# One-core pruned-weight matmul: another queue for the first token pair, one load in place of two for the first 512 weight columns, and a rewritten opening order

## The chip, the core and the metric

The kernel runs on one NeuronCore of a Trainium2 chip. The metric is the device time of one launch in microseconds (us). The kernel before was timed in three runs: 233.45, 233.73 and 233.89 us, median 233.73 us.

A core has five instruction streams that run side by side and meet only at semaphores: TensorE (PE in the profile, its weight loads PEld), VectorE (DVE), ScalarE (ACT), GpSimd (POOL) and SyncE (SP). SP, ACT and POOL can each issue DMA transfers; the transfers of all three run on the same 16 DMA engines.

## The reference

```python
def reference(x, w, b):                  # x 16x512x1024, w 1024x1024, b 1024, all bf16
    wg = w.reshape(G, M, D)              # M = 4 neighbouring rows of w form a group
    mag = jnp.abs(wg)
    order = jnp.argsort(mag, 1)
    thr = jnp.take_along_axis(mag, order[:, M - N:M - N + 1, :], 1)   # N = 2: the second largest
    mask = mag >= thr
    wp = (wg * mask).reshape(D, D)
    return jnp.einsum("bsd,df->bsf", x, wp) + b
```

In each column of w, out of every four neighbouring rows the two with the largest magnitudes are kept and the others become zero. Then 8192 tokens are multiplied by the pruned weights and the bias is added.

## The kernel before

**Tiles.** The 8192 tokens are 64 tiles of 128. The contraction (1024) is split in two halves g of 512, the output columns in two halves h of 512. A weight tile `w_gh[(g, h)]` has 128 partitions, 4 rows m (the four rows of a group, so that pruning works along the free dimension) and 512 columns. Pruning goes by six *pieces* (line 61): pieces 0 to 3 are the four 256-column quarters of g = 0, pieces 4 and 5 the two 512-column halves of g = 1.

**Pruning a piece.** `abs_piece` (lines 107 to 120) takes the magnitudes, on DVE or, with `on_act`, on ACT. `prep_piece` (lines 122 to 144) runs on DVE: maximum and minimum of row pairs (`hi`, `lo`, lines 129 and 130), three more to reach the threshold (lines 133, 134, 136), then the mask (line 142) and the product that overwrites w (line 144). For pieces 0 and 1 mask and product are done in two halves of two rows each, first both masks, then both products.

**The opening.** The first eight token tiles cannot wait for DMA transposes. They are loaded in pairs (`load_x`, line 76, 256 KB each), transposed on PE against an identity matrix (line 161; the identity is made on POOL, line 100), copied from PSUM to SBUF by ACT (`copy_half`, line 166), and multiplied by the pruned w where it lies (line 182). While the first loads are on their way, PE multiplies zeros (`warm`, line 103).

**The loads** are issued in the order of lines 83 to 90, and later ones by the order below. SP and ACT each issue their own list, one after another:

```python
    load_w(0, 0, 256, nc.sync, 0, 2)
    load_w(0, 0, 256, nc.scalar, 2, 4)
    load_x(0, 2)
    load_x(2, 4, nc.scalar)
    load_x(4, 6)
    load_w(0, 256, 512)
    load_x(6, 8)
    load_w(0, 512, 1024)
```

**The order.** `K` keeps the program order, so each engine executes its own instructions in the order in which they are written. The string `FRONT` (lines 256 to 268) writes the first tokens' work out by hand. Its words: W and w, a matmul of zeros with 512 or 128 columns; A.i and P.i, magnitudes and pruning of piece i; T.t and C.t, transposes of token tile t (four instructions) and its copy by ACT; M.i.t, the four matmuls of tile t with piece i; N.i.t.m.., only those of the rows m; V, a copy of a finished half sum from PSUM to SBUF on ACT; U, DMAs that move pruned w to the layout of the rest of the kernel (line 151); I, a weight load; D, G, L, DMA transposes of later tokens; X, Y, O, B, Q, the sums of the later front tiles, their additions and the bias load. All engines get their parts of this one list.

**The rest.** From line 328 on, 50 token tiles are multiplied by the whole pruned w, 16 matmuls of 512 columns each (line 338; the last tile by line 234), and DVE adds the bias while it empties PSUM (line 219).

Of the kernel before, what the change touches and what calls it, by code (L numbers as in the profile page):

```python
# [10 lines left out]
def kernel(  # L11
# [7 lines left out]
    nc = tc.nc  # L19
    P = 128  # L20
# [7 lines left out]
    B, S, D = x.shape  # L28
# [10 lines left out]
    T, F = 8, 6  # L39
# [13 lines left out]
    def next_bank():  # L53
        bk = nbk[0] % 8
        nbk[0] += 1
        return bk
# [8 lines left out]
    def w_of(i):  # L65
        g, c0, c1 = pieces[i]
        return w_gh[(g, c0 // FH)][:, :, c0 % FH:c0 % FH + c1 - c0]

    def load_w(g, c0, c1, eng=nc.sync, m0=0, m1=4):
        dst = w_gh[(g, c0 // FH)][:, m0:m1, c0 % FH:c0 % FH + c1 - c0]  # L70
        K(eng.dma_start(dst, wv[:, g, m0:m1, c0:c1]))  # L71
# [4 lines left out]
    def load_x(ta, tb, eng=nc.sync):  # L76
        xt = const.tile([P, tb - ta, KH], bf16, name=f"xh_{ta}")
        src = xf[ta * P:tb * P, 0:KH].rearrange("(t p) c -> p t c", p=P)
        K(eng.dma_start(xt[:], src))  # L79
        for t in range(ta, tb):  # L80
            xh[t] = xt[:, t - ta, :]

    load_w(0, 0, 256, nc.sync, 0, 2)
    load_w(0, 0, 256, nc.scalar, 2, 4)
    load_x(0, 2)
    load_x(2, 4, nc.scalar)
    load_x(4, 6)
    load_w(0, 256, 512)
    load_x(6, 8)
    load_w(0, 512, 1024)  # L90
    bias_sb = const.tile([P, Dout], bf16, name="bias_sb")
# [10 lines left out]
    def warm(n):  # L102
        K(nc.tensor.matmul(bank[7][:, :n], lhsT=zeros[:, :P], rhs=zeros[:, :n], start=True, stop=True))  # L103
# [3 lines left out]
    def abs_piece(i, on_act):  # L107
        g, c0, c1 = pieces[i]
        n = c1 - c0
        if n <= 256:  # L110
            mag = mags_pool.tile([P, 4, n], bf16, name="mag")[:]
        else:
            mag = mag2_pool.tile([P, 4, n], bf16, name="mag2")[:]
        if on_act:
            K(nc.scalar.activation(mag, w_of(i), Act.Abs))
        else:
            for ms in (slice(0, 2), slice(2, 4)) if i == 0 else (slice(0, 4),):
                K(nc.vector.tensor_single_scalar(  # L118
                    mag[:, ms].bitcast(u16), w_of(i)[:, ms].bitcast(u16), 0x7FFF, op=Alu.bitwise_and))
        mags[i] = mag  # L120

    def prep_piece(i):
        g, c0, c1 = pieces[i]
        n = c1 - c0
        mag = mags.pop(i)
        magv = mag.rearrange("p (a j) f -> p a j f", j=2)
        hi = tmp.tile([P, 2, FH], bf16, name="hi")[:, :, :n]
        lo = tmp.tile([P, 2, FH], bf16, name="lo")[:, :, :n]
        K(nc.vector.tensor_tensor(hi, magv[:, :, 0, :], magv[:, :, 1, :], op=Alu.max))
        K(nc.vector.tensor_tensor(lo, magv[:, :, 0, :], magv[:, :, 1, :], op=Alu.min))  # L130
        t1 = tmp.tile([P, FH], bf16, name="t1")[:, :n]
        t2 = tmp.tile([P, FH], bf16, name="t2")[:, :n]
        K(nc.vector.tensor_tensor(t1, hi[:, 0, :], hi[:, 1, :], op=Alu.min))
        K(nc.vector.tensor_tensor(t2, lo[:, 0, :], lo[:, 1, :], op=Alu.max))
        thr = tmp.tile([P, FH], bf16, name="thr")[:, :n]
        K(nc.vector.tensor_tensor(thr, t1, t2, op=Alu.max))
        mask = tmp.tile([P, 4, FH], bf16, name="mask")[:, :, :n]

        halves = (slice(0, 2), slice(2, 4)) if i < 2 else (slice(0, 4),)
        for ms in halves:  # L140
            tb = thr[:, None, :].to_broadcast([P, ms.stop - ms.start, n])
            K(nc.vector.tensor_tensor(mask[:, ms], mag[:, ms], tb, op=Alu.is_ge))  # L142
        for ms in halves:
            K(nc.vector.tensor_tensor(w_of(i)[:, ms], w_of(i)[:, ms], mask[:, ms], op=Alu.mult))  # L144

    wp_nat = [const.tile([P, KT, FH], bf16, name=f"wp_nat{h}") for h in range(2)]

# [8 lines left out]
    def transpose_half(t):  # L156
        own[(0, t)] = next_bank()
        xv = xh[t].rearrange("p (q m) -> p m q", m=4)
        dst = bank[own[(0, t)]][:].bitcast(bf16)[:, :4 * P].rearrange("p (m q) -> p m q", m=4)
        for m in range(4):  # L160
            K(nc.tensor.transpose(dst[:, m, :], xv[:, m, :], ident[:]))  # L161

    def copy_half(t):
        xt = const.tile([P, 4, P], bf16, name=f"xT_{t}")
        src = bank[own[(0, t)]][:].bitcast(bf16)[:, :4 * P].rearrange("p (m q) -> p m q", m=4)
        K(nc.scalar.copy(xt[:], src))  # L166
        xT[t] = xt


    def mm_part(q, t, c0, c1, ms=range(4)):  # L170
        g, h = divmod(q, 2)
        if c0 == 0 and (q > 0 or t >= T) and 0 in ms:
            own[(q, t)] = next_bank()
        dst = bank[own[(q, t)]][:, c0:c1]
        for m in ms:
            if t >= T:
                lhs, rhs = xN[t][:, 4 * g + m, :], wp_nat[h][:, 4 * g + m, c0:c1]
            elif g == 0:
                lhs, rhs = xT[t][:, m, :], w_gh[(0, h)][:, m, c0:c1]
            else:  # L180
                lhs, rhs = xg1[:, m, t * P:(t + 1) * P], wp_nat[h][:, 4 + m, c0:c1]
            K(nc.tensor.matmul(dst, lhsT=lhs, rhs=rhs, start=c0 == 0 and m == 0, stop=c1 == FH and m == 3))  # L182
# [45 lines left out]
    def load_fill(g):  # L228
        src = xf[T * P:(T + F) * P, g * KH:(g + 1) * KH]
        K(nc.sync.dma_start_transpose(out=xfill[:, 4 * g:4 * g + 4, :], in_=src))  # L230
# [6 lines left out]
    def issue_batch(t0, nb):  # L237
# [16 lines left out]


    FRONT = """
        I.1.0.512 D.0 A.0 P.0 W W W W W W W W w w T.0 T.1 C.0 T.2 T.3 C.1 w T.4 T.5 C.2 N.0.0.0 N.0.0.1 N.0.1.0
        N.0.1.1 N.0.0.2 N.0.0.3 N.0.1.2 N.0.1.3 A.1 C.3 P.1 U.0.0.0.512 I.1.512.1024 G C.4 M.0.2 C.5 M.0.3 T.6 T.7
        C.6 M.0.4 C.7 A.2 M.0.5 M.0.6 P.2 M.0.7 M.1.0 A.3 M.1.1 M.1.2 M.1.3 V.0.0 M.1.4 V.0.1 M.1.5 V.0.2 M.1.6
        V.0.3 M.1.7 V.0.4 P.3 M.2.0 V.0.5 M.2.1 V.0.6 M.2.2 V.0.7 M.2.3 M.2.4 M.2.5 M.2.6 A.4 P.4 U.1.0.0.512 D.1  # L260
        M.2.7 M.3.0 M.3.1 V.1.0 M.3.2 V.1.1 M.3.3 V.1.2 M.3.4 V.1.3 M.3.5 V.1.4 M.3.6 V.1.5 M.3.7 V.1.6 X.0.8 V.1.7
        X.0.9 V.0.8 X.0.10 V.0.9 X.0.11 V.0.10 X.0.12 V.0.11 X.0.13 V.0.12 V.0.13 A.5 P.5 U.1.1.0.512 U.0.1.0.512 Q
        L.0 L.1 N.4.0.0 N.4.1.0 N.4.2.0 N.4.3.0 N.4.0.1 N.4.1.1 N.4.2.1 N.4.3.1 N.4.0.2 N.4.1.2 N.4.2.2 N.4.3.2
        N.4.0.3 N.4.1.3 N.4.2.3 N.4.3.3 M.4.4 O.0.0 M.4.5 O.0.1 M.4.6 O.0.2 M.4.7 O.0.3 X.2.8 O.0.4 X.2.9 O.0.5
        X.2.10 O.0.6 X.2.11 O.0.7 X.2.12 O.0.8 X.2.13 O.0.9 N.5.0.0 N.5.1.0 N.5.0.1 N.5.1.1 N.5.0.2 N.5.1.2 N.5.0.3
        N.5.1.3 O.0.10 O.0.11 O.0.12 O.0.13 M.5.2 O.1.0 M.5.3 O.1.1 M.5.4 O.1.2 M.5.5 O.1.3 M.5.6 O.1.4 M.5.7 O.1.5
        O.1.6 O.1.7 Y.8 B.0.8 Y.9 B.0.9 Y.10 B.0.10 Y.11 B.0.11 Y.12 B.0.12 Y.13 B.0.13
    """
    for tok in FRONT.split():
        k, *n = tok.split(".")  # L270
        n = [int(c) for c in n]
        if k in "MN":
            g, c0, c1 = pieces[n[0]]
            h = c0 // FH
            mm_part(2 * g + h, n[1], c0 - h * FH, c1 - h * FH, n[2:] or range(4))
        elif k in "Ww":
            warm(FH if k == "W" else P)
        elif k == "A":
            abs_piece(n[0], 2 <= n[0] < 4)
        elif k == "P":  # L280
            prep_piece(n[0])
        elif k == "T":
            transpose_half(n[0])
        elif k == "C":
            copy_half(n[0])
        elif k == "Z":
            mm_part(n[0], n[1], 0, FH, n[2:])
        elif k == "I":
            load_w(*n)
        elif k == "D":  # L290
            load_fill(*n)
        elif k == "G":
            K(nc.sync.dma_start_transpose(out=xg1[:], in_=xf[0:T * P, KH:D]))
        elif k == "Q":
            for f in (slice(0, FH), slice(FH, Dout)):
                K(nc.sync.dma_start(bias_sb[:, f], b[f].partition_broadcast(P)))
        elif k == "X":
            mm_part(n[0], n[1], 0, FH)
        elif k == "V":
            to_stage(*n)  # L300
        elif k == "O":
            add_stage(*n)
        elif k == "B":
            add_bias(*n)
        elif k == "U":
            unpack(*n)
        elif k == "Y":
            bk = next_bank()
            mm_nat(n[0], 1, bk)
            evac_dve(n[0], 1, bk)  # L310
        elif k == "L":
            issue_batch(*batches[n[0]])
# [60 lines left out]
```

## Time and profile before

| | |
|---|---|
| runs (median of three) | 233.73 us |
| span of the profiled execution | 231.5 us |
| PE busy | 226.3 us, 98% of the span |
| DVE busy | 119.9 us, 52% |
| ACT busy | 18.8 us, 8% |
| POOL busy | 0.7 us |
| the costliest group, line 338 (737 matmuls of 512 columns) | 161.7 us |
| line 182, pieces 0 to 3 (128 matmuls of 256 columns) | 14.3 us |
| line 161, transposes (32 matmuls of 128 columns) | first at 4.96 us |
| first matmul with weights (line 182) | 6.84 us |
| last matmul ends | 228.66 us |

The profile is of one execution. The span goes from its first to its last instruction; the runs are timed from outside. The runs' median is 2.2 us above the span. A line of a group gives the source line, the engine, the operation, out<-in by the program's names, the shape, the number of instructions, then after the bar the busy time in us, the mean duration of one in ns, and the engine's idle time before them. Matmuls overlap: one with 512 columns lasts 379 ns from its start to its end, while in a stream they start about 216 ns apart.

### The profile page before, as it was taken

How to read it: one execution, taken by the hardware profiler on the slowest of the kernel's cores; microseconds unless marked ns; L12 is line 12 of the kernel's file. 1: busy time of each engine (PE TensorE's matmuls, PEld its weight loads, DVE VectorE, ACT ScalarE, POOL GpSimd, SP SyncE). 2: the span in 40 equal slices, each digit the busy share in tenths (PEclk: the TensorE clock that was granted, in tenths of full speed). 3: DMA queues.
4: the chain of work that ended last, by engine and by line, in shares of the span. 5: the costliest groups of instructions: out<-in, count | busy, mean ns of one | idle time of the engine just before them, and what ended most of it. 6: DMA issues, size and time to landing. Idle time of an engine off the chain costs nothing.

```text
span 231.5 us, 2724 instructions
## 1 busy us (share of the span) xinstructions
PE 226.3 (98%) x1128; PEld 110.6 (48%) x1147; DVE 119.9 (52%) x204; ACT 18.8 (8%) x34; POOL 0.7 (0%) x6
## 2 busy tenths in 40 slices
PE   7999999999999999999999999999999999999995
PEld 3887444444444444444444444444444444444443
DVE  4899887867987424424424423423433433433433
ACT  3977500000000000000000000000000000000000
POOL 1000000000000000000000000000000000000000
DMA  6999889999847221995239822696129991122222
GB/s 194 319 200 242 190 178 178 253 246 296 295 181 272 91 83 34 239 201 172 93 75 238 230 93 91 120 258 197 63 91 197 188 249 46 47 91 91 91 93 91
DMA packets 76972, 38.19 MB, mean 165 GB/s; under 512 B 62752, under 2 KB 68896, under 8 KB 76960
## 3 DMA queue, kind: packets, MB, share of 16 engines
q1 hardware_dynamic: 67696, 20.91, 45.2%
q10 hardware_dynamic: 9264, 17.11, 20.4%
q8 instruction: 9, 0.15, 0.3%
q14 instruction: 3, 0.02, 0.0%
HBM read 3.41 MB, written 16.78 MB: 87 GB/s over the span
## 4 chain that ended last, share of the span: by engine, by line
PE 96%; DMA 2%; issue 1%; SPq 0%; DVE 0%
PE bank L338 73%; PE bank L182 16%; PE bank L234 6%; DMA xh<-in_x_dram 2%; PE bank L161 0%; SPq L79 0%; SPq L71 0%; DVE o_last L323 0%
## 5 line engine op out<-in xcount | busy, mean ns | idle before, releaser
L338 PE MATMUL bank<-wp_nat,xTb 128*128 128x512 bf16 x737 | 161.7, 379 | 0.8
L219 DVE TENSOR_TENSOR o_pair<-bank,bias_sb 128x512 bf16<-128x512 f32 x104 | 67.3, 686 | 99.6 <-PE bank L338 94.2
L338 PEld LDWEIGHTS <-xTb 128*128 128x128 bf16 x752 | 73.6, 98 | 88.7
L210 DVE TENSOR_TENSOR stage<-bank,stage 128x512 f32<-128x512 f32 x22 | 14.4, 686 | 3.9 <-PE bank L182 3.8
L182 PE MATMUL bank<-w,xT 128*128 128x256 bf16 x128 | 14.3, 273 | 0.0
L214 DVE TENSOR_TENSOR o_pair<-stage,bias_sb 128x512 bf16<-128x512 f32 x22 | 14.0, 682 | 0.0
L182 PE MATMUL bank<-wp_nat,xg 128*128 128x512 bf16 x62 | 13.9, 379 | 0.1
L182 PEld LDWEIGHTS <-xT 128*128 128x128 bf16 x128 | 12.5, 98 | 1.4
L206 ACT COPY stage<-bank 128x512 f32<-128x512 f32 x22 | 11.4, 618 | 3.9 <-PE bank L182 3.9
L182 PE MATMUL bank<-wp_nat,xfill 128*128 128x512 bf16 x47 | 10.6, 379 | 0.1
L234 PE MATMUL bank<-wp_nat,xfill 128*128 128x512 bf16 x47 | 10.5, 379 | 0.1
L182 PEld LDWEIGHTS <-xg 128*128 128x128 bf16 x64 | 6.3, 98 | 7.6
L234 PEld LDWEIGHTS <-xfill 128*128 128x128 bf16 x48 | 4.7, 98 | 5.7
L182 PEld LDWEIGHTS <-xfill 128*128 128x128 bf16 x48 | 4.7, 98 | 5.5
L338 PE MATMUL bank<-wp_nat,xTs 128*128 128x512 bf16 x32 | 7.1, 379 | 0.0
L142 DVE TENSOR_TENSOR mask<-mag,thr 128x512 bf16<-128x512 bf16 (+2 forms) x8 | 5.4, 690 | 0.2
L144 DVE TENSOR_TENSOR w<-w,mask 128x512 bf16<-128x512 bf16 (+2 forms) x8 | 5.3, 688 | 0.1
L103 PE MATMUL bank<-zeros 128*128 128x512 bf16 (+1 forms) x11 | 4.0, 533 | 1.2 <-DVE zeros L96 1.2
L338 PEld LDWEIGHTS <-xTs 128*128 128x128 bf16 x32 | 3.1, 98 | 3.8
L166 ACT COPY xT<-bank 128x512 bf16<-128x512 bf16 x8 | 4.1, 607 | 2.7 <-PE bank L161 2.7
L118 DVE TENSOR_SCALAR mag<-w 128x512 uint16<-128x512 uint16 (+2 forms) x5 | 2.3, 477 | 2.7 <-DMA w<-in_w_dram 2.7
L234 PE MATMUL bank<-wp_nat,xTb 128*128 128x128 bf16 (+2 forms) x32 | 3.7, 272 | 0.0
(20 smaller groups left out, 26.9 us busy)
## 6 DMA issues: line engine op xcount, KB each, us to landing
out_dram<-o_pair ACTq DMA_DIRECT2D x31, 512.0 KB, 2.8
wp_nat<-w SPq DMA_DIRECT2D x16, 128.0 KB, 2.8
w<-in_w_dram SPq DMA_DIRECT2D x3, 512.0 KB, 6.0
xh<-in_x_dram SPq DMA_DIRECT2D x3, 256.0 KB, 4.5
xh<-in_x_dram ACTq DMA_DIRECT2D x1, 256.0 KB, 4.0
w<-in_w_dram SPq DMA_DIRECT2D x1, 256.0 KB, 5.1
bias_sb<-in_b_dram SPq DMA_DIRECT2D x2, 128.0 KB, 3.7
out_dram<-o_pair ACTq DMA_DIRECT2D x1, 256.0 KB, 2.0
```

The lines of the kernel that those rows point to most:

```text
L103: K(nc.tensor.matmul(bank[7][:, :n], lhsT=zeros[:, :P], rhs=zeros[:, :n], start=True, stop=True))
L118: K(nc.vector.tensor_single_scalar(mag[:, ms].bitcast(u16), w_of(i)[:, ms].bitcast(u16), 0x7FFF, op=Alu.bitwise_and))
L142: K(nc.vector.tensor_tensor(mask[:, ms], mag[:, ms], tb, op=Alu.is_ge))
L144: K(nc.vector.tensor_tensor(w_of(i)[:, ms], w_of(i)[:, ms], mask[:, ms], op=Alu.mult))
L166: K(nc.scalar.copy(xt[:], src))
L182: K(nc.tensor.matmul(dst, lhsT=lhs, rhs=rhs, start=c0 == 0 and m == 0, stop=c1 == FH and m == 3))
L206: K(nc.scalar.copy(stage[(h, t)][:], bank[own[(h, t)]][:]))
L210: K(nc.vector.tensor_tensor(st, bank[own[(2 + h, t)]][:], st, op=Alu.add))
L214: K(nc.vector.tensor_tensor(get_o(t)[:, f], stage.pop((h, t))[:], bias_sb[:, f], op=Alu.add))
L219: K(nc.vector.tensor_tensor(get_o(t)[:, f], bank[bk][:], bias_sb[:, f], op=Alu.add))
L234: K(nc.tensor.matmul(bank[bk][:, :c1 - c0], lhsT=xN[t][:, kt, :], rhs=wp_nat[h][:, kt, c0:c1], start=kt == 0, stop=kt == KT - 1))
L338: K(nc.tensor.matmul(bank[bks[h]][:], lhsT=xN[t][:, kt, :], rhs=wp_nat[h][:, kt, :], start=kt == 0, stop=kt == KT - 1))
```

## The change

Four things change.

- **Loads.** The first 512 columns of w come in one step: SP loads rows 0 and 1, ACT rows 2 and 3 (256 KB each; before 128 KB each for 256 columns, and the other 256 columns in a load of their own, fourth on SP's list). The first token pair is issued by POOL, where it stands ahead of the two instructions that make the identity matrix; before, SP issued it second.
- **Magnitudes.** Those of piece 1 are taken on ACT, and stand in its list ahead of all copies of transposes; before, DVE took them.
- **Pruning of piece 0.** Each half's product follows its mask.
- **Order.** One matmul of zeros with 512 columns fewer, two with 128 columns more. All 32 transposes come before the first matmul with weights; before, the last eight came after sixteen such matmuls. Pieces 0 to 2 are partly multiplied by two rows at a time, in an order in which a tile's first two rows come some steps before its last two. The work itself, apart from the zeros, has the same instructions.

```diff
-    load_w(0, 0, 256, nc.sync, 0, 2)
-    load_w(0, 0, 256, nc.scalar, 2, 4)
-    load_x(0, 2)
+    load_w(0, 0, 512, nc.sync, 0, 2)
+    load_w(0, 0, 512, nc.scalar, 2, 4)
+    load_x(0, 2, nc.gpsimd)
     load_x(2, 4, nc.scalar)
     load_x(4, 6)
-    load_w(0, 256, 512)
     load_x(6, 8)
     load_w(0, 512, 1024)
...
-        for ms in halves:
+        def keep(ms):
             tb = thr[:, None, :].to_broadcast([P, ms.stop - ms.start, n])
             K(nc.vector.tensor_tensor(mask[:, ms], mag[:, ms], tb, op=Alu.is_ge))
-        for ms in halves:
+
+        def prune(ms):
             K(nc.vector.tensor_tensor(w_of(i)[:, ms], w_of(i)[:, ms], mask[:, ms], op=Alu.mult))
+
+        halves = (slice(0, 2), slice(2, 4)) if i < 2 else (slice(0, 4),)
+        if i == 0:
+            for ms in halves:
+                keep(ms)
+                prune(ms)
+        else:
+            for ms in halves:
+                keep(ms)
+            for ms in halves:
+                prune(ms)
...
-        I.1.0.512 D.0 A.0 P.0 W W W W W W W W w w T.0 T.1 C.0 T.2 T.3 C.1 w T.4 T.5 C.2 N.0.0.0 N.0.0.1 N.0.1.0
-        N.0.1.1 N.0.0.2 N.0.0.3 N.0.1.2 N.0.1.3 A.1 C.3 P.1 U.0.0.0.512 I.1.512.1024 G C.4 M.0.2 C.5 M.0.3 T.6 T.7
-        C.6 M.0.4 C.7 A.2 M.0.5 M.0.6 P.2 M.0.7 M.1.0 A.3 M.1.1 M.1.2 M.1.3 V.0.0 M.1.4 V.0.1 M.1.5 V.0.2 M.1.6
+        I.1.0.512 D.0 A.0 A.1 P.0 W W W W W W W w w w w T.0 T.1 C.0 T.2 T.3 w T.4 C.1 T.5 w C.2 T.6 T.7 C.3
+        N.0.0.0.1 N.0.1.0.1 C.4 N.0.2.0.1 N.0.3.0.1 P.1 U.0.0.0.512 I.1.512.1024 G N.0.0.2.3 C.5 N.0.4.0.1
+        N.0.1.2.3 C.6 N.0.5.0.1 N.0.2.2.3 C.7 N.0.3.2.3 N.0.6.0.1 A.2 N.0.4.2.3 N.0.7.0.1 N.0.5.2.3
+        N.0.6.2.3 N.0.7.2.3 A.3 N.1.0.0.1 P.2 N.1.0.2.3 M.1.1 V.0.0 M.1.2 V.0.1 M.1.3 V.0.2 M.1.4 N.1.5.0.1
...
-            abs_piece(n[0], 2 <= n[0] < 4)
+            abs_piece(n[0], 1 <= n[0] < 4)
```

## The prediction

> **What bounds the kernel now.** I read the share of each engine first, then the chain that ended last, then the opening in order of time, then the stretches of DMA traffic.
>
> ```profile
> PE 226.3 (98%) x1128; PEld 110.6 (48%) x1147; DVE 119.9 (52%) x204; ACT 18.8 (8%) x34; POOL 0.7 (0%) x6
> ```
>
> TensorE is busy almost all the time, so only its idle or useless time can be won. The chain shows where that is:
>
> ```profile
> 1.74 4.53 DMA xh<-in_x_dram
> 6.28 0.05 issue
> 6.32 0.64 PE bank L161 x8
> 6.96 1.79 PE bank L182 x16
> 8.75 0.45 PE bank L161 x8
> 9.19 13.31 PE bank L182 x117
> ```
>
> The columns are start, length and what. The chain leaves PE only at the third token pair, which lands at 6.28; from 6.32 to the end it is PE without a break. So the change can act only through the opening: whatever moves the moment from which PE works without a break moves the end by as much, unless a new stall follows. PE's own list:
>
> ```profile
> 1.19 3.81 PE L103 MATMUL bank<-zeros 128*128 128x512 bf16 x10 [1.19 <-DVE zeros L96]
> 4.96 1.17 PE L161 MATMUL bank<-ident,xh 128*128 128x128 bf16 x16
> ...
> 6.32 0.64 PE L161 MATMUL bank<-ident,xh 128*128 128x128 bf16 x8
> 6.84 1.91 PE L182 MATMUL bank<-w,xT 128*128 128x256 bf16 x16
> 8.58 0.61 PE L161 MATMUL bank<-ident,xh 128*128 128x128 bf16 x8
> 9.03 12.39 PE L182 MATMUL bank<-w,xT 128*128 128x256 bf16 x112
> 21.25 1.03 PE L182 MATMUL bank<-wp_nat,xfill 128*128 128x512 bf16 x4
> ```
>
> At 9.03 it has done all 32 transposes and 16 weight matmuls. The 112 that follow take 21.25 - 9.03 = 12.22 us, 0.109 each. In the changed order all 32 transposes come first, so if its first weight matmul starts at S and nothing stalls, it stands at the same point at S + 16 x 0.109 = S + 1.75. **The change costs S - 7.28 us.** S is the later of two things: the last token pair transposed, and half of piece 0 pruned.
>
> **The token pairs: bytes.** How fast the DMA engines work (the last two columns are their mean busy share and GB/s; over 1 where packets overlap):
>
> ```profile
> 2.00:2.50 0.50, 0.50 (x3) 0.21 (x2) 0.00 (x0) 0.50 (x1) 0.00 (x0) 1.00 0.34 88
> 2.50:4.50 2.00, 2.00 (x6) 0.68 (x5) 0.86 (x3) 0.77 (x2) 0.00 (x0) 1.00 1.11 361
> 4.50:6.25 1.75, 1.68 (x20) 1.20 (x18) 1.68 (x7) 0.76 (x2) 0.00 (x0) 1.00 0.93 284
> 6.25:7.25 1.00, 0.93 (x12) 0.89 (x13) 0.87 (x3) 1.00 (x3) 0.00 (x0) 1.00 1.11 365
> 7.25:9.25 2.00, 2.00 (x25) 1.84 (x24) 1.84 (x6) 1.52 (x4) 0.00 (x0) 1.00 1.10 358
> ```
>
> From 2.5 on the engines are full. So a third queue and shorter lists (SP issues the last pair two places earlier, saving two issues of 0.45 to 0.68) change the order of arrival, not the sum. Ahead of the last pair stand the same bytes as before: w 0.52 MB and four pairs of 0.26, 1.57 MB. Before, 0.05 had gone by 2.5, 0.77 by 4.5, 1.27 by 6.25, and 1.57 at 7.1; the pair, issued at 2.97 with 5.1 us to landing, landed at 8.1, so 1.0 after its bytes were due. The first pair (1.24 + 3.7 = 4.9) came 0.35 after its 0.79 MB. What the change gains is the slack stretch, 284 instead of some 360, in which the fourth load ran with 512-byte rows; its rows are now 1024 bytes. At 360 throughout, the remaining 1.52 MB take 4.2 us and end at 6.7. With a lag of 0.35 to 1.0 the last pair lands between 7.05 and 7.7; I take 7.45, a little above the middle, since it is last in line on the most loaded queue, as before. From the landing at 6.28 to the first weight matmul at 6.84, with eight transposes between, took 0.56. So this bound on S is **8.0** (7.6 to 8.3).
>
> **Piece 0: w.** Before, the later half of w was issued at 0.73 and landed 3.1 us later, at 3.8; the first weight matmul stood 3.0 behind it, through this chain:
>
> ```profile
> 3.61 0.52 DVE L118 TENSOR_SCALAR mag<-w 128x512 uint16<-128x512 uint16 x2 [2.48 <-DMA w<-in_w_dram]
> ...
> 5.69 0.76 DVE L142 TENSOR_TENSOR mask<-mag,thr 128x512 bf16<-128x512 bf16 x2
> 6.37 0.75 DVE L144 TENSOR_TENSOR w<-w,mask 128x512 bf16<-128x512 bf16 x2
> ```
>
> With product behind mask, the first product no longer waits for the second mask (0.76 - 0.42 = 0.34) but now directly for its own mask, which costs the overlap of neighbours, about 0.12: 2.8 instead of 3.0. But w now brings twice the bytes, beside the first pair on POOL's queue. If that pair takes a full share, 0.79 MB go by 4.55 and w lands at 4.9; if it comes too late to share, 0.52 MB go by 3.8 and w lands at 4.15. I take 4.8, near the full share, since all three are issued at once. Half of piece 0 is then pruned at **7.6** (6.95 to 7.7), before the transposes are done. So the faster pruning and the larger load are hidden behind the last pair; without that cover they would set S = 7.6, 0.3 later than level.
>
> **The rest, and what hides it.** The POOL load has no row before. From issue to landing the nearest rows are 2.9 (SP's w) and 6.0 (SP's 512 KB load): 3.6 to 6.7. I take 4.9, as for the pair on SP's list. Up to about 6.3 it costs nothing, since the transposes of three pairs (24 x 0.056, 1.35) fit before the last pair is there; at 6.7 it costs 0.3. The identity behind it on POOL was ready at 1.3; the nearest issue rows are 0.45 and 0.68, so 2.0, needed at about 4.9. The magnitudes of piece 1 on ACT take 1.06 (the row of pieces 2 and 3) and wait for both halves of w: 4.8 to 5.9. Behind them stand eight copies, 0.48 apart. PE needs the fourth at S + 0.65 = 8.65, and it comes at about 8.0; the fifth at S + 1.1, about 8.5. Piece 1 follows piece 0 on DVE, which ends 3.5 after w (8.3); its first half took 2.6 before, from `hi` at 7.80 to the product's end at 10.42, so it is there at 10.9, needed after 32 weight matmuls at S + 3.5 = 11.5. Piece 2: ready at 14.2 (2.9 behind piece 1's end at 11.3, as before), needed at S + 7.0 = 15.0. Later pieces keep DVE's old pace while PE comes later, so their slack grows; the unpack U.0.0 can go at 11.3, and went at 11.75 before, when SP's 6.7 us issue of a transposing DMA held it. The zeros end at 4.57 instead of 4.79 and only fill a wait. So the sum is S - 7.28 = 8.0 - 7.28 = **+0.7 us**. The profiled execution's span would be 232.2 instead of 231.5; the runs lie 2.2 above the span, so 233.73 + 0.7 = **234.4**.
>
> **Rivals.**
>
> *Level.* The last pair lands with the smallest lag, or early bytes on the third queue fill part of the ramp before 2.5 (88 GB/s). S = 7.3 to 7.7, 233.8 to 234.2, about 234.0. For it: lag 0.35 was seen. Against: the lag grew with every load before.
>
> *Faster.* POOL's descriptors reach idle DMA engines before SP's do, from about 1.3, and the engines run at 365 from then on. 1.57 MB end at 5.6, the pair lands at 6.0, and w (0.79 MB) at 3.85, so pruning sets S = 6.65 to 6.75: -0.55, **233.2**. It decides if w lands before 4.0. Against: SP's first load, issued at 0.73, had moved 0.05 MB by 2.5. The Trainium skill (DMA: Bandwidth & Descriptors, "Specifications") gives a first byte after about 1 us on GpSimd's path and 0.6 on SP's and ACT's; by that this rival is out. No row here shows POOL's queue.
>
> *Slow clock.* The zeros run at half the later pace: the first row of PE's list is 8 x 512 + 2 x 128 columns in about 3.5 us, 0.8 ns a column, against 0.42 in 12.22 us for 112 x 256. The change of pace falls into the first transposes, about 4 us after the start (the profile's granted clock, 1.00, doesn't show it). If the pace depends on PE having been busy, the new opening is weaker: zeros end at 4.57, then 8 transposes, then a wait for the second and third pair until about 6.5. If the full pace comes only 4 us after 6.5, then PE works at half pace from 8.0 to 10.5, +1.25 more: **235.6**. It decides if PE idles more than it works between 4.6 and 6.5. Against: 0.17 and 0.3 us of idling before did no harm. The Trainium skill (TensorE: Matmul & The Clock Gate, "What's actually happening") has this as a free-running window of about 3.4 us whose activity sets the clock, with full pace only after a busy one. Its threshold is not told; by it the switch could come up to 6.5 + 3.4 = 9.9, an estimate from that figure of up to +0.95.
>
> *Late first pair.* It lands at 6.7 or later, or the identity does: S = 8.3 to 9, **235.0**.
>
> **How the numbers follow.** About 0.2% (0.47 us) is what a measurement can tell here. Forecast 0.54, of which 0.09 below that bound; level 0.20; faster 0.07; slow clock 0.12; late pair 0.07. Slower: 0.45 + 0.12 + 0.07 = 0.64. Same: 0.09 + 0.20 = 0.29. Faster 0.07. The range 233.8 to 235.5 leaves out the faster case, the edge of level, and over half of the slow clock.
>
> **What would show it.** Right: the first weight matmul at 7.6 to 8.3, directly behind the transposes of the last pair, whose landing ends PE's last idle time; no gap after it; DMA share near 1.1 until then, at about 360 GB/s. Wrong: the first weight matmul waits for DVE (w was the later), or for the copies; transposes or weight matmuls at half pace after 5.5; the last pair landing before 7.0; or a gap before piece 1 or 2.

## The result and the profile after

The changed kernel takes **237.59 us** (median of 5 runs, 236.43 to 237.82) against 233.62 (233.44 to 233.89, 5 runs beside it) before: 3.97 us more, ratio over all runs 1.0156 with a 95% interval of 1.0136 to 1.0176 (the quotient of the medians, 1.0170, lies inside). The direction was forecast, the size was not: 234.4 us had been forecast, 3.2 less than came.

The profiled execution took 237.82 us with a span of 236.0. Its row of the engines, to hold against the first line of the prediction:

```profile
PE 228.7 (97%) x1130; PEld 112.9 (48%) x1149; DVE 119.6 (51%) x203; ACT 19.9 (8%) x35; POOL 1.5 (1%) x7
```

The span is 4.5 us longer. PE was busy for 2.4 us more of it, with two instructions more (of the zeros, one matmul with 512 columns fewer and three with 128 more, one more than I had counted): part of the loss is waiting, and part is the same work done slower. Its own list (start, length, what; in brackets the idle time ahead and what ended it):

```profile
1.20 3.59 PE L102 MATMUL bank<-zeros 128*128 128x512 bf16 x11 [1.20 <-DVE zeros L95]
6.93 1.90 PE L171 MATMUL bank<-ident,xh 128*128 128x128 bf16 x16 [2.14 <-DMA xh<-in_x_dram]
...
8.73 1.06 PE L171 MATMUL bank<-ident,xh 128*128 128x128 bf16 x8
...
9.69 1.06 PE L171 MATMUL bank<-ident,xh 128*128 128x128 bf16 x8
10.54 13.67 PE L192 MATMUL bank<-w,xT 128*128 128x256 bf16 x113
```

Three things are to be read here. PE waits 2.14 us for the *first* token pair, not for the last. Eight transposes take 1.06 us, where the same eight took 0.64 and 0.61 before (their starts lie 0.107 apart instead of 0.056), and that holds for all 32; the zeros ahead of the wait are as slow, those of 512 columns start 0.427 apart against 0.216 in a stream. And the first weight matmul, S of the prediction, starts at 10.54, not at 8.0. Behind it the weight matmuls start 0.213 apart until 12.95, then 0.109 as before, and PE has no gap to its end: its last matmul ends at 233.08 instead of 228.66, 4.42 later.

The DMA stretches, in the columns the prediction gave (last two: busy share of the engines, GB/s):

```profile
2.50:4.50 2.00, 2.00 (x9) 0.90 (x7) 0.39 (x2) 0.87 (x3) 0.15 (x1) 1.00 1.01 340
4.50:6.25 1.75, 0.29 (x3) 0.02 (x1) 1.66 (x6) 0.97 (x1) 0.00 (x0) 1.00 1.07 364
6.25:7.25 1.00, 0.32 (x4) 0.33 (x5) 0.96 (x3) 0.00 (x0) 0.00 (x0) 1.00 1.08 364
```

The slack stretch from 4.5 to 6.25 is full now, 364 GB/s instead of 284, just as forecast. But PE, the first column behind the length, is busy for 0.29 of 1.75 us and 0.32 of 1.00 us, where it had 1.68 and 0.93 before: the bytes go at full rate, in an order that leaves PE without work. POOL's list shows the load that PE waits for:

```profile
1.24 0.83 POOL L79 DMA_DIRECT2D xh<-in_x_dram  x1 [0.79 <-POOLq L370]
2.07 0.22 POOL masks.py:197 MEMSET ident<- 128x128 bf16 x1
2.37 0.29 POOL masks.py:199 TENSOR_SCALAR_AFFINE_SELECT ident<-ident 128x128 bf16<-128x128 bf16 x1
```

It is issued at 1.24, POOL is busy with it to 2.07, and it lands at 6.88, 5.6 us after its issue. The first packet on POOL's queue is at 5.05. The queues up to that moment (packets, MB, share) and in the stretch behind it:

```profile
q1 hardware_dynamic: 539, 0.52, 33.1%
q10 hardware_dynamic: 462, 0.46, 25.6%
```

```profile
q1 hardware_dynamic: 351, 0.35, 54.6%
q0 software_dynamic: 80, 0.26, 41.4%
q10 hardware_dynamic: 82, 0.07, 11.0%
```

q1 is SP's, q10 ACT's, q0 POOL's. When POOL's queue moves its first packet, 0.98 MB of the others have gone: both halves of w and nearly two token pairs. The pair that PE needs first comes third: ACT's pair landed at 6.03, SP's at 5.62, the last at 7.54.

One warning on the chain that ended last. It runs through ACT and DVE here:

```profile
1.24 5.64 DMA xh<-in_x_dram
6.93 0.63 PE bank L171 x4
7.58 4.01 ACT xT L176 x8
```

and reaches PE for good only at 37.77, through a transfer of pruned weights. Yet PE has no idle time between 6.93 and 37.77: those waits ended just when PE was ready. The list of PE's idle times decides, not the chain.

### The profile page after: what moved, and what is told of

Its sections match the earlier page's. It is cut to its first block, busy times and chain, and to the rows that moved or that the text cites. A ratio compares the mean times of both kernels' runs of the same rounds, so it can differ in the third digit from the quotient of the medians.

```text
span 236.0 us, 2730 instructions
## 1 busy us (share of the span) xinstructions
PE 228.7 (97%) x1130; PEld 112.9 (48%) x1149; DVE 119.6 (51%) x203; ACT 19.9 (8%) x35; POOL 1.5 (1%) x7
## 3 DMA queue, kind: packets, MB, share of 16 engines
HBM read 3.41 MB, written 16.78 MB: 86 GB/s over the span
## 4 chain that ended last, share of the span: by engine, by line
PE 83%; DVE 5%; SPq 5%; DMA 3%; ACT 2%; issue 1%; POOLq 0%
PE bank L351 71%; PE bank L244 6%; PE bank L192 5%; SPq L161 3%; DMA xh<-in_x_dram 2%; ACT xT L176 2%; SPq L240 1%; DVE mask L140 1%; DVE w L143 1%; DMA wp_nat<-w 1%; DVE hi L128 1%; DVE lo L129 1%; DVE thr L135 0%; ACT mag L114 0%; DVE t L133 0%
## 5 line engine op out<-in xcount | busy, mean ns | idle before, releaser
L192 PE MATMUL bank<-w,xT 128*128 128x256 bf16 x128 | 15.3, 285 | 0.0
L192 PEld LDWEIGHTS <-xT 128*128 128x128 bf16 x128 | 13.1, 103 | 2.0
L171 PE MATMUL bank<-ident,xh 128*128 128x128 bf16 x32 | 3.8, 311 | 2.1 <-DMA xh<-in_x_dram 2.1
L171 PEld LDWEIGHTS <-xh 128*128 128x128 bf16 x32 | 3.4, 145 | 2.4 <-DMA xh<-in_x_dram 2.4
```

## The experiments

Theory: the late first pair costs part of the 4 us directly, and the idle time that it makes costs the rest through PE's slow pace. Rivals: the new order or the heavier first load costs it; POOL's path has a fixed delay; the slow pace comes from something other than idling.

**e1_pair0_on_sp: the change with its first pair back on SP.**

```diff
-    load_x(0, 2, nc.gpsimd)
+    load_x(0, 2)
```

> The changed kernel with the first token pair back on SP's list, second, as before; all else as changed. Theory (the late pair costs everything: its landing at 6.88 and the slow matmul pace that follows from PE's idle time): the pair lands at 5.0 to 5.6, no slow matmuls after 6, the first weight matmul at about 8.1 directly behind the last pair, 234.3 to 234.7 us. Rival 1 (the slow pace comes from the new opening order whatever queue is used): slow transposes and weight matmuls remain, 235.3 to 236.5. Rival 2 (the larger first weight load and the order cost it): 236.4 or more with fast matmuls.

Measured: 234.38 us against 233.38, ratio 1.0045 (1.0029 to 1.0062): +1.0, so the other parts of the change, POOL's load apart, cost 1.0. PE's list:

```profile
5.32 1.88 PE L171 MATMUL bank<-ident,xh 128*128 128x128 bf16 x16 [0.53 <-DMA xh<-in_x_dram]
...
7.28 0.64 PE L171 MATMUL bank<-ident,xh 128*128 128x128 bf16 x8
...
8.04 0.64 PE L171 MATMUL bank<-ident,xh 128*128 128x128 bf16 x8
```

The first sixteen transposes are slow too, but lie ahead of the third pair's landing (7.23), and cost nothing. S is 8.51, set by the last pair's landing at 7.99, and 8.51 - 7.28 = 1.23 is how much later the last matmul ends (229.89 against 228.66). Two of twelve runs were at 235.8; the trace is of another one. e11 below, the same opening with another order on SP's list, took 235.46 with a slow pace until 9.75, which is a likely reason and not a shown one.

**e2_before_pool: before, with POOL's load alone.**

```diff
-    load_x(0, 2)
+    load_x(0, 2, nc.gpsimd)
```

> The kernel before with one edit: the first token pair issued by POOL. Theory (the DMA engines take transfers roughly in the order in which their descriptors are ready, and POOL's are ready only at the end of its 0.8 us issue): the pair stands behind the two w halves and two other pairs, 0.79 MB, and lands at 5.5 to 5.9; PE idles about 1 us and the end moves by 0.6 to 0.9, plus up to 2 if the slow pace lasts: 234.2 to 236.5. Rival (a fixed delay of POOL's queue, about 3 us from the end of its issue to the first packet, whatever else runs): it lands at about 6.9 again, end later by 1.6 plus up to 2.9: 235.2 to 238.

Measured: 236.41 against 233.38, ratio 1.0113 (1.0084 to 1.0142): +3.03. With e1's 1.00 that makes 4.03, about the whole loss (3.97). That is support and no proof: e2's runs lie between 234.73 and 237.04, and POOL's pair is 0.6 later here than in the change. The first packet came at 4.45, when 0.75 MB of the others had gone; that is what was issued ahead of it here (two w loads of 0.13 and two pairs of 0.26, 0.79). But the pair landed at 7.52, 1.6 to 2 later than I expected and later than the rival's 6.9, and the total lies in both ranges. So this run alone does not decide between the two; the bytes ahead tell when the transfer begins and not when it ends.

**e3_more_zeros: the change with eight more matmuls of zeros** ahead of the transposes, nothing else.

```diff
-        I.1.0.512 D.0 A.0 A.1 P.0 W W W W W W W w w w w T.0 T.1 ...
+        I.1.0.512 D.0 A.0 A.1 P.0 W W W W W W W W W W W W W W W w w w w T.0 T.1 ...
```

> The changed kernel with 15 instead of 7 matmuls of zeros with 512 columns, so that PE is busy until about the first pair's landing at 6.9. Theory (PE's idle time from 4.6 to 6.9 keeps the slow matmul pace until about 12.9, which costs 2.9 us of the 4.4): the transposes run 0.056 apart, weight matmuls 0.109, the first weight matmul at about 8.9, 235.1 to 235.5 us. Rival (the pace has another cause, or the late pair alone costs all): 236.4 to 237.8 as without the zeros.

Measured: 234.99 against 233.38, ratio 1.0060 (1.0041 to 1.0079): of the 3.97 us over before, 1.61 are left. Work that computes nothing wins back 2.4. PE's list:

```profile
1.20 5.27 PE L102 MATMUL bank<-zeros 128*128 128x512 bf16 x19 [1.20 <-DVE zeros L95]
6.74 1.08 PE L171 MATMUL bank<-ident,xh 128*128 128x128 bf16 x16 [0.27 <-DMA xh<-in_x_dram]
...
7.71 0.61 PE L171 MATMUL bank<-ident,xh 128*128 128x128 bf16 x8
```

The pair is as late as in the change (6.69), and the transposes go at full pace: S = 8.66. This splits the loss. All of the change but the pace costs 234.99 - 233.38 = 1.6, and the pace the other 2.4. Of the 1.6, e1 has 1.0 without the late pair; so the late pair at full pace adds some 0.6 by the medians (in the two profiled executions the last matmul ends only 0.25 later).

**e4_quiet_pool: nothing ahead of POOL's load.** In the changed kernel ACT first writes zeros over the tile of w, so that SP's and ACT's loads wait.

```diff
...
+    for j in range(4):
+        K(nc.scalar.copy(w_gh[(0, 0)][:, j, :], zeros[:]))
...
     load_w(0, 0, 512, nc.sync, 0, 2)
     load_w(0, 0, 512, nc.scalar, 2, 4)
```

> A measurement of POOL's load with the DMA engines idle: the changed kernel, in which ACT first writes zeros over the first w tile, so that both w loads and all loads listed behind them wait until about 5 us; the zeros are overwritten by the loads, nothing of the result changes. Theory (order of arrival: it was late because 1.05 MB stood ahead of it): from issue to landing 2.9 to 3.6 us instead of 5.6. Rival (a fixed delay of POOL's queue): 5 us or more. The total is expected about 4 us above the changed kernel and decides nothing.

Measured (one run): 240.66. The line of the load in the trace:

```profile
DMA to landing us min/median/max: 3.2/3.2/3.2
```

From the same issue at 1.24 it lands 3.2 later instead of 5.6, with a first packet at 2.79 instead of 5.05. The rival of a fixed delay falls: 2.4 us of the 5.6 come with the transfers of the others.

**e5_ident_first: POOL's load behind the identity.**

```diff
-    load_x(0, 2, nc.gpsimd)
...
     make_identity(nc, ident[:])
+    load_x(0, 2, nc.gpsimd)
```

> The changed kernel with the identity matrix made first on POOL, so that POOL's load is issued some 0.6 us later. Theory (order of arrival: a transfer is worked off behind those whose descriptors were ready before its own): POOL's load now falls behind the last pair of SP's list too; its first packet comes at 5.9 or later instead of 5.05, it lands at 7.4 to 8.0, and the last pair lands earlier, at 6.8 to 7.1 instead of 7.54. Rival (POOL's queue just needs about 3 us while the others are busy): first packet about 0.6 later (5.6), landing about 7.4, and the last pair stays at 7.5. The total, 237.5 to 239, decides nothing.

Measured (one run): 237.37. The issue came only 0.19 later (1.43), yet the first packet 0.64 later (5.69, with 1.16 MB gone: part of the last pair had got ahead). It landed at 7.63. I had expected the last pair clearly ahead of it, at 6.8 to 7.1; it landed at 7.83, so the two shared the engines. First packet and landings lie nearer to the rival's figures (5.6, 7.4 and 7.5) than to the theory's. What speaks against a fixed wait of about 3 us is the other runs: from the end of POOL's issue to its first packet passed 0.7 us in e4, 1.4 in e9, 2.4 in e2, 3.0 in the change and 3.4 here, the longer the more bytes had been issued ahead. What this run shows best is the pace:

```profile
7.67 1.08 PE L171 MATMUL bank<-ident,xh 128*128 128x128 bf16 x16 [2.88 <-DMA xh<-in_x_dram]
...
8.66 1.06 PE L171 MATMUL bank<-ident,xh 128*128 128x128 bf16 x8
```

Sixteen transposes right after an idle time of 2.88 us go at full pace, and the eight behind them take as long as the sixteen. The slow pace lasts from 8.6 to 12.0 and ends by itself. So it does not follow the idle time at once: it comes later and lasts some 3.4 us. The granted clock, the third column from the end, shows the same:

```profile
5.22:8.63 3.41, 0.96 (x17) 0.96 (x18) 3.27 (x12) 0.85 (x3) 0.00 (x0) 1.00 1.03 350
8.63:12.04 3.41, 3.41 (x29) 2.98 (x27) 2.20 (x8) 3.41 (x9) 0.00 (x0) 0.50 1.22 273
```

**e6_e1_more_zeros: e1 with three more matmuls of zeros.**

```diff
-        I.1.0.512 D.0 A.0 A.1 P.0 W W W W W W W w w w w T.0 T.1 ...
+        I.1.0.512 D.0 A.0 A.1 P.0 W W W W W W W W W W w w w w T.0 T.1 ...
```

> The changed kernel with the first pair on SP's list and 10 instead of 7 matmuls of zeros with 512 columns, so that PE works until about the pair's landing at 5.3. Theory (the later runs of the version with 7, 235.8 in two of twelve, are executions in which the slow matmul pace lasted longer because PE idled): all runs within 234.1 to 234.6, transposes 0.056 apart. Rival (that spread is chance of the measurement): single runs near 235.8 again.

Measured: 234.36 against 233.32, ratio 1.0041 (1.0029 to 1.0053), S at 8.52 as in e1. Where the slow stretch is hidden, zeros win nothing. On e1's two long runs it decides nothing: none of five here, two of twelve there.

**e7_before_3_zeros: before with five matmuls of zeros fewer**, loads and queues unchanged.

```diff
-        I.1.0.512 D.0 A.0 P.0 W W W W W W W W w w T.0 T.1 ...
+        I.1.0.512 D.0 A.0 P.0 W W W w w T.0 T.1 ...
```

> The kernel before with 3 instead of 8 matmuls of zeros with 512 columns, so that PE idles from about 2.7 to 5.0; loads and order as before. Theory (PE's idle time alone keeps the slow pace for some 4 us more): slow transposes and weight matmuls until 8 to 10, 234.3 to 235.6 us. Rival (the slow pace in the changed kernel came from POOL's load): within 0.3 of the kernel before.

Measured: 234.63 against 233.32, ratio 1.0066 (1.0045 to 1.0086).

```profile
5.00 1.89 PE L161 MATMUL bank<-ident,xh 128*128 128x128 bf16 x16 [2.13 <-DMA xh<-in_x_dram]
...
6.79 1.06 PE L161 MATMUL bank<-ident,xh 128*128 128x128 bf16 x8
```

The same 2.13 us of idling, made without POOL and with the pair landing as before (4.95 against 4.91), give the same slow transposes, until 8.4. With e3 this shows it from both sides: with the idle time the slow pace lasts longer, and with zeros in its place it ends sooner. In both, as in the change, the first zeros are slow too; so here the idle time delays the full pace and does not take it away.

**e8_before_one_load: before with the first 512 columns in one step**, its fourth load dropped, its order kept.

```diff
-    load_w(0, 0, 256, nc.sync, 0, 2)
-    load_w(0, 0, 256, nc.scalar, 2, 4)
+    load_w(0, 0, 512, nc.sync, 0, 2)
+    load_w(0, 0, 512, nc.scalar, 2, 4)
...
-    load_w(0, 256, 512)
```

> The kernel before with one edit: the first 512 columns come in one load of two row halves, on SP and ACT, and the fourth load is dropped; queue of the first pair, magnitudes and order as before. Theory (the doubled first load pushes all pairs back, and the third pair's landing, not the order, sets the start): the third pair lands at about 7.2 instead of 6.3 and the end moves by 0.6 to 1.0: 234.0 to 234.4. Rival (the new order, with all transposes first, costs the microsecond of the version with the first pair on SP): 233.3 to 233.7.

Measured: 234.13 against 233.32, ratio 1.0030 (1.0019 to 1.0041): +0.8. In the profiled execution the first, third and last pair landed at 5.75, 7.18 and 7.93; that execution is the longest of the eight (235.79, the others 233.91 to 234.18), with 0.80 us of idling and a slow pace until 10.28. The median's +0.8 is most of e1's 1.0, so the heavier first load costs it rather than the new order: the bytes of w that piece 1 needs much later now stand ahead of the tokens that PE needs first.

**e9_pool_third: the change with POOL's load ahead of the two other pairs.** POOL clears 16 columns in the tiles of the second and third pair, so that their loads wait for it.

```diff
         xt = const.tile([P, tb - ta, KH], bf16, name=f"xh_{ta}")
+        if ta in (2, 4):
+            K(nc.gpsimd.memset(xt[:, :, :16], 0.0))
```

> The changed kernel, in which POOL, after issuing its load, clears 16 columns of the second and third pair's tiles, so that SP's and ACT's loads of them are issued only after POOL's (the loads overwrite the zeros; the result is unchanged). Theory (the DMA engines work transfers off in the order in which their descriptors were ready): only the two w halves, 0.52 MB, stand ahead of POOL's load; its first packet comes at 3.3 to 3.9 instead of 5.05, it lands at 4.6 to 5.2, PE idles under 0.7 us before the first transposes, the first weight matmul comes at 8.1 to 8.6 and the run takes 234.1 to 234.9, with single runs a microsecond higher. Rival (POOL's queue is served about 3 us after its issue whenever the other queues have work): first packet at about 5, landing at 6.5 or later, 235.5 to 237.8.

Measured: 237.87 against 233.68, ratio 1.0170 (1.0152 to 1.0189). The first packet came at 3.44, as the order of arrival has it (0.48 MB of the others had gone), but the pair landed at 6.32, not at 4.6 to 5.2. The total missed its forecast (234.1 to 234.9) as well: the second pair, held back by the edit, came only at 8.44, PE sat idle for 1.57 and 1.07 us, S was 11.24 and the slow pace lasted until 13.6. The DMA stretches around it:

```profile
3.50:4.25 0.75, 0.75 (x4) 0.24 (x2) 0.38 (x2) 0.74 (x3) 0.00 (x0) 1.00 1.07 335
4.25:6.00 1.75, 0.55 (x5) 0.28 (x3) 1.66 (x6) 0.97 (x1) 0.00 (x0) 1.00 0.77 216
```

The engines' share falls to 0.77 and the rate to 216 GB/s while POOL's pair is on its way: the first of the 16 engines was done with its part of the pair at 4.52, the last at 6.32. Why POOL's transfer ends so unevenly stays open.

**e10_before_late_d and e11_e1_late_d: SP's transposing DMA later**, in before and in e1. The slack stretch of before (284 GB/s) might come from its 6.7 us issue on SP and not from the 512-byte rows. The edit in before's order (in e1's, D.0 goes behind the same U):

```diff
-        I.1.0.512 D.0 A.0 P.0 ...
+        I.1.0.512 A.0 P.0 ...
...
-        ... A.1 C.3 P.1 U.0.0.0.512 I.1.512.1024 ...
+        ... A.1 C.3 P.1 U.0.0.0.512 D.0 I.1.512.1024 ...
```

> The kernel before with the first transposing DMA (D.0) moved behind the unpack U.0.0 on SP's list. Theory (SP's issue of the transposing DMA, which takes 7 us from about 4.9, makes the DMA engines take up the loads already listed more slowly): the stretch from 4.5 to 6.25 moves 330 GB/s or more instead of 284 and the third pair lands at 5.7 to 6.0 instead of 6.3. Rival (the slack has another cause): 270 to 300 and 6.2 to 6.5. The rest of the kernel gets its fill tokens later; the total decides nothing.

> The changed kernel with the first pair on SP's list and the first transposing DMA (D.0) moved behind the unpack U.0.0. Theory (as in the other run): the stretch from 4.5 to 6.25 moves 340 GB/s or more instead of 302, and the last pair lands at 7.3 to 7.7 instead of 8.0. Rival: about 300 and 7.9 to 8.1. The total decides nothing.

Measured (one run each): 233.64 against 233.46, and 235.46. In e10 the third pair landed at 6.55, later than theory and rival had it. e11's 235.46 is the pace again: 0.79 us of idling, transposes 0.107 apart, S = 9.18. The stretch in before without that issue:

```profile
4.50:6.25 1.75, 1.52 (x20) 1.12 (x18) 1.68 (x6) 0.92 (x2) 0.00 (x0) 1.00 0.93 265
```

The same stretch in e1 and, below it, in e1 without that issue:

```profile
4.50:6.25 1.75, 1.22 (x12) 0.95 (x11) 1.65 (x7) 1.08 (x2) 0.00 (x0) 1.00 0.94 302
```

```profile
4.50:6.25 1.75, 0.96 (x10) 0.70 (x9) 1.68 (x6) 1.02 (x2) 0.00 (x0) 1.00 1.05 347
```

In before the stretch stays slack, in e1 it fills, and in e1 the last pair lands no earlier for it (7.92 against 7.99). So neither cause is shown, and the answer differs between the two kernels. All bytes up to the last pair's (1.57 MB) had gone by about 6.8 in e11, and the pair landed 1.1 us later: the first of the 16 engines was done with its part of it at 6.86, the last at 7.92. The mean rate does not tell when that is.

## Why the prediction was wrong, by its steps

**The account held.** "The change costs S - 7.28 us" would give 3.26 for S = 10.54; the 11 weight matmuls behind it that took 0.213 instead of 0.109 add 1.14, together 4.40 against 4.42 measured at the last matmul. No stall followed S, as forecast.

**The step that failed: POOL's load.** "From issue to landing the nearest rows are 2.9 … and 6.0 …: 3.6 to 6.7. I take 4.9 … Up to about 6.3 it costs nothing." It landed at 6.88. My bounds took the rows of SP's loads, counted from an issue at 0.73 (POOL's came at 1.24), and not what would stand ahead of this one. The price was short too: by the prediction's own terms a pair at 6.7 gives S = 6.7 + 1.35 + 0.56 = 8.6, which is 0.6 and not 0.3 late, and the cover ends at 6.1. With the pair at 6.69, e3 has 8.66. So a load that was entered at nothing cost 3.0 us by the medians: some 0.6 directly and 2.4 through the pace.

The prediction noted that engines were full from 2.5 on and that the third queue changes only "the order of arrival"; it did not work that order out. POOL's issue is done only at 2.07, when SP and ACT have issued both halves of w and both next pairs: 4 x 0.262 = 1.05 MB. Counting each packet of POOL's by the bytes of the others that had gone, its median packet stands at 1.05 MB in the change, 1.05 in e3, 0.79 in e2 (where 0.79 stood ahead) and 0.52 in e9 (0.52 ahead): the list of what was issued first gives it in these four. In e5, where the last pair's issue also ended just before POOL's, it stands at 1.24, between 1.05 and 1.31. With the end of the issue known, which no row of before shows, the prediction's own numbers give the time: with the pair itself that is 1.31 MB, which were gone at about 6.4 before (1.27 by 6.25, then 365 GB/s), and with its lag of 0.35 to 1.0 the pair lands at 6.7 to 7.4, in no case early enough to cost nothing. The same sum fails for e9 and e2, whose pairs landed later than it has them; so it gives the start and a lower bound, and that it fits the landing in the change is partly luck.

The Trainium skill (DMA: Bandwidth & Descriptors, "Queues, rings and completion order") has each engine go round between the queues, a packet's worth from each. By that POOL's packets would have mixed with the others' from the start; the runs show a first packet only after most of the earlier bytes were gone (0.75 MB in e2, 0.98 in the change, 1.16 in e5), and they decide here. Whether its descriptors were ready earlier and waited their turn, or were not yet there, no run shows.

**The late pair's price held.** The rival of that name was "S = 8.3 to 9, 235.0", chance 0.07. With the pair nearly as late (6.69) and full pace (e3) it is S = 8.66 and 234.99. Of that, 1.0 us over before is there without the late pair (e1).

**The slow clock: mechanism right, size and link wrong.** Its mechanism was named (zeros end at 4.57, then PE waits, and the full pace comes only some 4 us later), and so was its condition, "if PE idles more than it works between 4.6 and 6.5". But it was priced as a rival beside the late pair, at +1.25 for weight matmuls alone. The late pair is what makes the condition so plainly true: PE idled from 4.8 through all of that stretch. And the transposes, entered at 0.056 throughout, go at 0.107: 34 instructions (32 and two of zeros) x 0.051 = 1.7 in the profiled execution, on top of 1.14. In the medians the pace costs 2.4. The two rivals were one case, worth 234.99 + 2.4 = 237.4, and no chance in the prediction stood for it.

In the change the profile's granted clock says 1.00 throughout, because its trace has no clock record; there only the distance between starts shows the pace. Where there are records they agree with it: in e5 the clock is 1.00 from 5.22 and 0.50 from 8.63 to 12.04. The Trainium skill (TensorE: Matmul & The Clock Gate, "What's actually happening") has a free-running window of 3.4 us whose activity sets the next one's clock. e5 agrees (0.50 for 3.41 us).

The change itself was slow from its first zeros to 12.95, whenever PE was at work. The traces tell roughly how busy a window must be. Counted in steps of 3.41 us back from the moment of full pace (the start of the first clock record, or the change of spacing in before, the change and e9, which have none), PE was busy for 84% to 100% of each window after which a slow pace became full, in all 13 profiles, and for at most 77% of each after which it stayed slow (61% and 76% in the change, 77% in e8 and e11). A pace already full outlasted windows of 73% (e6) and 83% (e10) and was lost after 28% (e5), 19% (e4) and 16% (e2). Where the windows lie differs from run to run: with the same seven zeros of 512 columns the full pace came at 12.95 in the change, 9.75 in e11, 7.04 in e1 and 5.22 in e5, though e5's pair was the latest. So part of a single run's time is luck.

**The last pair's landing** was entered as 7.45 (7.05 to 7.7). It was 7.54 in the change, where POOL's pair arrives beside it, but 7.99 with that pair on SP (e1), and so what stands for the forecast's own +0.7 measured +1.0. In the change the sum of bytes came out: they were gone at 6.7, as forecast, and the lag was 0.8. In e1 they were gone at 6.9 and the lag was 1.1, just over the 0.35 to 1.0; the stretch of 284 was 302 there although its rows have 1024 bytes, and filling it (e11) moved the last landing by 0.07.

**What held:** w landed at 4.39 (4.8 forecast, 4.15 to 4.9) and half of piece 0 was pruned 2.76 later (2.8 forecast), hidden behind the transposes; the identity was ready at 2.66 (2.0 forecast), with cover; pieces 1 and 2 and the copies had slack (piece 2 was pruned 4.7 behind piece 1; the prediction's "2.9 …, as before" misreads a row, it was 3.2 before), and the first weight matmul came directly behind the transposes.

**Open:** why POOL's transfer has such a long tail (2.9 us from first packet to landing in e9, 3.1 in e2), what filled or emptied the stretch from 4.5 to 6.25, and where between 77% and 84% of a window the pace turns full. None of the versions tried is faster than before.

## What to carry to other kernels

When a load moves to another queue, price it by what has been issued ahead of it on *all* queues by the moment its own issue is done, and let the transfer begin only behind those bytes; then add a lag for the slowest DMA engine, which for POOL's load was up to 3 us here. Whatever PE waits for first must be issued first, and bytes that are needed later (here the second half of w) must not be put ahead of it. If a change lets PE idle for a microsecond or two in the opening, price the idle time and the slow pace behind it as one case, and fill a wait that can't be avoided with matmuls of zeros until the data are sure to be there: eight of them were worth 2.4 us here.

## What was not expected of the hardware

- POOL's first load could be issued only at 1.24, SP's and ACT's at 0.74. It moved its first packet 1.55 us after its issue on idle engines (e4: 1.24 to 2.79), and 3.8 us after it with the other queues at work (1.24 to 5.05).
- 0.19 us of delay in its issue became 0.64 us at its first packet (e5), by when 0.18 MB more of the other loads had gone.
- From the time at which all bytes ahead of and in the last pair had gone to its landing, 1.0 us passed in before and 1.1 in e11, with the 16 engines' mean share near 1.
- PE's pace fell to half for 3.4 us in e5 almost a microsecond after work had begun again (transposes from 7.67 at full pace, slow from 8.6). In the change it never reached full before 12.95, though PE was at work from 1.20 to 4.79 and from 6.93 on.
